# First feed-forward in pieces of 384 tokens across pairs of batches, weight products in rows of 16 array tiles, and new plan times

## The chip, the cores and the metric

The kernel runs on one core of one Trainium2 chip. The metric is the device time of one execution in microseconds (us). The engines of the core are TensorE (PE in the rows; PEld is its weight load), VectorE (DVE), ScalarE (ACT), GpSimd (POOL) and SyncE (SP); the last two also issue transfers.

## The reference

Three stages follow each other. Packed attention: 32 learned queries `p` attend to 576 keys of each head, and the 576 queries attend to the 32 results. Then two feed-forwards run over 8 x 576 = 4608 tokens of width 512.

```python
# B, H, S, D = 8, 8, 576, 64; 32 packed queries
p_packed = softmax(p @ k.T / 8) @ v
out = softmax(q @ p_packed.T / 8) @ p_packed
x = out.transpose(0, 2, 1, 3).reshape(4608, 512)
h = x @ w_in                            # 512 x 2048
x = (h * sigmoid(1.702 * h)) @ w_out    # 2048 x 512
h = max(x @ w1, x @ w2, x @ w3)         # 512 x 768 each
out = h @ w_out2                        # 768 x 512
```

All data are fp32.

## The kernel before

**Precision.** A matmul in fp32r is done three times, on high and low parts of both operands: `mm3` (lines 111 to 115) issues low x high, high x low and high x high into one PSUM bank. Each of the three has its own weight load. Matmuls on plain fp32 data (scores, `pv`, `pw`) run as two passes on TensorE.

**Attention.** A `Group(b, g)` is four heads of a batch. Its small matmuls use a part of the array, 64 rows by 32 columns. Its result `at[b, g]` is not the attention's output but the second softmax (32 weights per head), transposed and split in high and low. The product with the packed values is moved into the weights: `pw_unit` (line 449) multiplies the packed values `sp[b, g]` of a batch with a quarter `n` of `w_in` (512 of 2048 hidden features) and so makes `pw[b, n]`, which the first feed-forward uses in place of `w_in`. A call makes this for both batches of a pair and one head group `g`: eight matmuls of 64x32 array tiles, one PSUM bank of 512 columns for each batch from the pool `ps_a` (two banks, tag `pa`). ScalarE copies a bank out as the high part, VectorE subtracts for the low part (`evac`, line 145). For pair 0, `wi` is the converted weight; for later pairs it is fetched again from DRAM by `load_wi` on GpSimd's queue into one of four `x` tiles.

**First feed-forward.** A unit `n` is a piece of tokens by 128 hidden features. `h_unit` (line 514) makes h for the piece with two `mm3`, one per head group, in one of two banks of `ps_h` (tag `ph`), and applies the GELU; `g_unit` splits it; `out_unit` (line 542) does four `mm3` into the four banks `c0` to `c3` of `ps_c`, which collect over the units of a run. A piece is half a batch, `HALF` = 288 tokens, so a batch has 32 units and the stage has 256. `PAT` and `PP` (lines 481 to 501) set the runs; batches 0, 1 and 7 are cut in runs of hidden features whose parts are added by VectorE (line 559). A finished run goes to DRAM (`x2d`) in one transfer.

**Order.** The order is a plan: `add(t, fn)` notes a step with a time in us that is only a key, and at the end all steps are sorted by it and issued (line 1022). The tables at the top (lines 33 to 48) set these times; `tn[n]` is the planned time of unit `n`. The output of unit `n-2` stands behind h of unit `n`. The weight products of a quarter are planned `Q_` or `R_` units ahead of their first use, the two head groups one or three units apart (lines 945 to 952). Engines run their instructions in the order issued.

**Second feed-forward.** It runs from about 749 us to the end, over blocks of 768 tokens, with weights that `Piece` (line 604) converts and combines during the late units of the first. Its matmuls have 384 columns (`p` in the rows) and 512 (`accb`).

Of the kernel before, what the change touches and what calls it, by code (L numbers as in the profile page):

```python
# [8 lines left out]
F32 = mybir.dt.float32  # L9
# [16 lines left out]
NFC = DFF // P  # L26
NF2 = DFF2 // P
# [17 lines left out]
B4_ = [20, 9.69, 1.29, 38.74]
PC_ = [-5.59, 5.97, 8.06, 6.97, 10.65, 15.48, 10.04, 11.93]
G_ = [15, 33, 97, 136, 183]
X_ = [252, 2.6]
PAIR0 = 1


@with_exitstack
def tile_packed_attention_moe(
# [395 lines left out]
    def pw_unit(bs, pr, g, n):  # L449
        w = wi[pr, g, n]  # L450
        os = {}
        for b in bs:
            if (b, n) not in pw:
                pw[b, n] = w_tile(f"pw_{b}_{n}")
            os[b] = pa_tile(f"pw_{b}_{g}_{n}")
# [8 lines left out]
        for b in bs:  # L464
            o = os[b]
# [7 lines left out]


# [17 lines left out]
    PP = []  # L492
    for b in range(2, B, 2):
        PP += {
            0: [(b, 0, 16), (b + 1, 0, 16)],
            1: [(x, y, y + 4) for x in (b, b + 1) for y in range(0, 16, 4)],
            2: [(x, y, y + 8) for x in (b, b + 1) for y in range(0, 16, 8)],
            3: [(x, y, y + 8) for y in range(0, 16, 8) for x in (b, b + 1)],
            4: [(x, y, y + 4) for y in range(0, 16, 4) for x in (b, b + 1)],
        }[0]  # L500
    PP[-1:] = [(B - 1, x, x + 4) for x in range(0, 16, 4)] if 4 == 4 else [(B - 1, x, x + 8) for x in range(0, 16, 8)] if 4 == 8 else PP[-1:]
    for b, f0, f1 in PAT + PP:
# [372 lines left out]
    def main():  # L875
# [204 lines left out]
```

## Time and profile before

| | before |
|---|---|
| median of 3 runs | 1297.01 us (1295.29 to 1297.29) |
| profiled execution, its own time | 1295.06 us |
| span from the first to the last instruction | 1293.3 us |
| granted TensorE clock, mean | 0.997 |
| TensorE matmuls | 1272.8 us busy (98%), 9990 |
| VectorE, ScalarE, GpSimd busy | 841.8, 522.7, 78.2 us |

The span is what one execution shows between its first and last instruction; the execution's own time is 1.8 us more. A busy share says that some instruction of the engine was under way. TensorE's rows overlap, since a matmul starts while the one before it still drains, so the distance between starts tells the pace. All rows are of the one profiled execution, with times in us from the span's start.

### The profile page before, as it was taken

What the parts mean: (1) busy time and instruction counts of PE and PEld (TensorE: products, weight loads), DVE (VectorE), ACT (ScalarE), POOL (GpSimd) and SP (SyncE); (2) the same over time, 40 slices, a digit from 0 to 9 for tenths busy, and PEclk for the clock granted to TensorE, in tenths of its full rate; (3) what the DMA queues carried; (4) which work ended last, traced back from release to release, by engine and by line L of the source; (5) the groups of instructions that cost most, each with busy time, mean ns of one, the idle gap of its engine ahead of it and who ended that gap; (6) DMA issues with size and microseconds to landing.
All of it is one profiled execution on the core that took longest, in us unless ns stands there. A gap on an engine that the chain in (4) does not pass through costs nothing.

```text
span 1293.3 us, 24741 instructions
## 1 busy us (share of the span) xinstructions
PE 1272.8 (98%) x9990; PEld 1179.7 (91%) x9990; DVE 841.8 (65%) x1734; ACT 522.7 (40%) x1133; POOL 78.2 (6%) x153
## 2 busy tenths in 40 slices
PE   6999999999999999999999999999999999999998
PEld 5688888899989899999999999899899999998997
DVE  7998788565543466588789887557467366366561
ACT  3676654454654454455556532312213123113111
POOL 1000000000000000000000011011011011010100
PEclk8999999999999999999999999999999999999999
DMA  8898254323220231045557399567477477474541
GB/s 311 315 406 314 74 157 145 103 88 99 91 87 18 90 109 48 24 145 182 170 180 240 129 347 342 202 218 245 157 260 250 156 260 247 160 254 177 187 172 49
DMA packets 84402, 233.07 MB, mean 180 GB/s; under 512 B 9792, under 2 KB 38976, under 8 KB 77376
## 3 DMA queue, kind: packets, MB, share of 16 engines
q1 hardware_dynamic: 64128, 115.62, 26.0%
q0 software_dynamic: 20160, 115.88, 25.8%
q8 instruction: 78, 1.28, 0.4%
q14 instruction: 36, 0.29, 0.1%
HBM read 191.88 MB, written 39.58 MB: 179 GB/s over the span
## 4 chain that ended last, share of the span: by engine, by line
PE 88%; DVE 5%; DMA 3%; ACT 2%; issue 1%; SPq 0%; DVEq 0%; ACTq 0%
PE p L115 10%; PE p L114 10%; PE p L113 10%; PE acc L113 10%; PE acc L115 9%; PE acc L114 9%; PE h L113 5%; PE h L115 4%; PE h L114 4%; PE accb L115 4%; PE accb L114 4%; PE accb L113 4%; PE pw L460 2%; PE s L311 1%; DMA wraw_o<-in_w_out 1%; PE pv L366 1%
## 5 line engine op out<-in xcount | busy, mean ns | idle before, releaser
L113 PE MATMUL acc<-g,wo 128*128 128x288 f32 x1024 | 309.0, 302 | 1.9 <-DVE x L559 1.4
L115 PE MATMUL acc<-g,wo 128*128 128x288 f32 x1024 | 301.1, 294 | 0.0
L114 PE MATMUL acc<-g,wo 128*128 128x288 f32 x1024 | 299.4, 292 | 0.0
L113 PEld LDWEIGHTS acc<-g,wo 128*128 128x128 f32 x1024 | 192.2, 188 | 32.3 <-ACT t L526 11.9
L115 PEld LDWEIGHTS acc<-g,wo 128*128 128x128 f32 x1024 | 192.0, 188 | 1.4 <-issue 1.3
L114 PEld LDWEIGHTS acc<-g,wo 128*128 128x128 f32 x1024 | 192.3, 188 | 0.6 <-issue 0.5
L113 PE MATMUL h<-at,pw 128*128 128x288 f32 x512 | 154.0, 301 | 1.2 <-ACT at L142 0.6
L114 PE MATMUL h<-at,pw 128*128 128x288 f32 x512 | 151.5, 296 | 0.4 <-DVE at L143 0.4
L115 PE MATMUL h<-at,pw 128*128 128x288 f32 x512 | 151.3, 296 | 0.0
L113 PE MATMUL p<-x_T,ws 128*128 128x384 f32 x324 | 108.2, 334 | 0.0
L114 PE MATMUL p<-x_T,ws 128*128 128x384 f32 x324 | 108.2, 334 | 0.0
L115 PE MATMUL p<-x_T,ws 128*128 128x384 f32 x324 | 108.1, 334 | 0.0
L750 DVE TENSOR_TENSOR u<-s,p 128x384 f32<-128x384 f32 x54 | 29.9, 554 | 118.3 <-PE p L115 118.3
L113 PEld LDWEIGHTS h<-at,pw 128*128 128x128 f32 x512 | 96.1, 188 | 9.7 <-issue 5.0
L534 DVE TENSOR_TENSOR g<-t,g 128x288 fp32r<-128x288 f32 x130 | 58.9, 454 | 67.9 <-ACT g L533 67.0
L524 ACT ACTIVATE t<-h 128x288 f32<-128x288 f32 x130 | 53.3, 410 | 112.5 <-PE h L115 112.1
L114 PEld LDWEIGHTS h<-at,pw 128*128 128x128 f32 x512 | 96.1, 188 | 1.6 <-DVE t L527 0.8
L115 PEld LDWEIGHTS h<-at,pw 128*128 128x128 f32 x512 | 96.1, 188 | 0.5 <-issue 0.5
L780 ACT COPY s<-p 128x384 f32<-128x384 f32 x54 | 25.9, 480 | 164.5 <-PE p L115 164.5
L527 DVE SCALAR_TENSOR_TENSOR t<-t,h 128x288 f32<-128x288 f32 x126 | 56.8, 451 | 54.1 <-ACT t L526 53.4
L526 ACT ACTIVATE t<-h 128x288 f32<-128x288 f32 x126 | 51.8, 411 | 93.2 <-PE h L115 92.7
L115 PE MATMUL accb<-wo,g 128*128 128x512 f32 x216 | 84.1, 390 | 0.0
(166 smaller groups left out, 2587.7 us busy)
## 6 DMA issues: line engine op xcount, KB each, us to landing
ws<-wss POOLq DMA_DIRECT2D x54, 1024.0 KB, 7.5
wa<-wsa POOLq DMA_DIRECT2D x54, 768.0 KB, 4.6
wi<-wsc POOLq DMA_DIRECT2D x24, 512.0 KB, 3.7
k<-in_k SPq DMA_DIRECT2D x16, 576.0 KB, 4.0
q<-in_q SPq DMA_DIRECT2D x16, 576.0 KB, 4.1
x2d<-x SPq DMA_DIRECT2D x16, 576.0 KB, 3.6
wss<-ws SPq DMA_DIRECT2D x36, 256.0 KB, 2.9
xr<-x2d SPq DMA_DIRECT2D x24, 384.0 KB, 4.3
```

The source lines that it names most:

```text
L113: nc.tensor.matmul(o, al, bh, start=start, stop=False, skip_group_check=more)
L114: nc.tensor.matmul(o, ah, bl, start=False, stop=False, skip_group_check=more)
L115: nc.tensor.matmul(o, ah, bh, start=False, stop=stop, skip_group_check=more)
L311: self.mm = nc.tensor.matmul(o[hf][rows(c, r, hf ^ self.swap), :HALF], w(c, rows_in(r)), x[rows_in(r), c, hf * HALF:hf * HALF + HALF], sta ...
L366: self.mm = nc.tensor.matmul(o[h][m, :D], self.et[rows_in(h), c * P + NP * j:c * P + NP * j + NP], self.v[rows_in(h), c, d:d + D], start=c ...
L460: nc.tensor.matmul(os[b][rows(x, r, b & 1)], sp[b, g][rows_in(r), NP * c:NP * c + NP], w[rows_in(r), c], start=True, stop=True,)
L524: latest["act"] = nc.scalar.activation(t, o, AF.Gelu_apprx_sigmoid)
L526: nc.scalar.activation(t, o, AF.Tanh, scale=0.5 * 1.702)
L527: nc.vector.scalar_tensor_tensor(out=t, in0=t, scalar=1.0, in1=o, op0=ALU.add, op1=ALU.mult)
L534: latest["dve"] = nc.vector.tensor_tensor(out=g[:, 1], in0=gt[n], in1=f(g[:, 0]), op=ALU.subtract)
L750: latest["dve"] = nc.vector.tensor_tensor(out=o, in0=a, in1=b, op=op)
L780: latest["act"] = nc.scalar.copy(self.s1, self.b1)
```

## The change

- From batch 2 on the pieces of the first feed-forward are windows of `WIDE` = 384 tokens over a pair of batches: two batches of 576 tokens are three pieces. The middle piece holds the last 192 tokens of one batch and the first 192 of the other. As the two batches have different `pw`, its h is made in two parts of 192 columns in one bank; its output matmuls have 384. The units become 64 of 288 (batches 0 and 1, as before) and 144 of 384, 48 of these with h in two parts: 208 instead of 256. Per pair and chunk of 128 hidden features that is 60 matmuls instead of 72.
- The last two pieces are done in turns of four chunks each, with parts added by VectorE. A finished piece fills two `x` tiles and goes out in two transfers.
- `pw_both` issues the matmuls of both head groups behind each other, the first into the banks of `ps_a`, the second into those of `ps_h`, and copies all four banks out after that. It stands behind h of a unit and the output of the unit two before; the output of the unit just before is drawn ahead and stands directly behind it (`early`), and two h units follow each other later.
- `load_wi` is planned 10 and 8 units ahead of the product instead of 7.
- All plan times are new: conversions (`K_`, `L_`), attention of batch 0 (`D_`), the start of the units (`T_`), the weights of the second feed-forward (`TP_`, `PC_`), the units whose GELU is one ScalarE instruction (`G_`), and places that were unit numbers (`X_`, `U_`).

```diff
+WIDE = 384
-Q_ = [9, 8, 9, 8]
-R_ = [18, 26, 14, 8]
+Q_ = [6, 8, 7, 7]
+R_ = [14, 24, 12, 8]
-T_ = [41.76, 1.21, 1.17, 7]
+T_ = [40.26, 1.21, 1.17, 10]
...
+    def h_tile(name):
+        return ps_h.tile([P, TB], F32, tag="ph", name=name)
...
-    def pw_unit(bs, pr, g, n):
+    def pw_unit(bs, pr, g, n, tile_=pa_tile):
...
-            os[b] = pa_tile(f"pw_{b}_{g}_{n}")
+            os[b] = tile_(f"pw_{b}_{g}_{n}")
...
+        return lambda: pw_out(os, g, n)
+
+    def pw_out(os, g, n):
+        for b, o in os.items():
...
+    def pw_one(*a):
+        pw_unit(*a)()
+
+    def pw_both(bs, pr, n):
+        for done in [pw_unit(bs, pr, g, n, (pa_tile, h_tile)[g]) for g in range(2)]:
+            done()
...
+    def window(c0, width):
+        parts = []
+        for b in range(c0 // S, (c0 + width - 1) // S + 1):
+            t0, t1 = max(0, c0 - b * S), min(S, c0 + width - b * S)
+            parts.append((b, t0, t1 - t0, b * S + t0 - c0))
+        return c0, width, tuple(parts)
+
+    for b, f0, f1 in PAT:
         for hf in range(2):
...
+    runs = [(x, 0, NFC) for x in range(2 * S, NT, WIDE)]
+    runs[-2:] = [(x, y, y + 4) for y in range(0, NFC, 4) for x in range(NT - 2 * WIDE, NT, WIDE)]
...
     def h_unit(n):
-        b, hf, fc = units[n]
-        o = ps_h.tile([P, TB], F32, tag="ph", name=f"h_{n}")[:, :HALF]
+        (_, width, parts), fc = units[n]
+        o = ps_h.tile([P, TB], F32, tag="ph", name=f"h_{n}")[:, :width]
...
-        for g in range(2):
-            w = pw[b, fc // 4][:, g]
-            mm3(o, (w[:, 0, fs], w[:, 1, fs]), [t[:, hs] for t in at[b, g]], g == 0, g == 1)
+        for b, t0, num, to in parts:
+            for g in range(2):
+                w = pw[b, fc // 4][:, g]
+                mm3(
+                    o[:, to:to + num], (w[:, 0, fs], w[:, 1, fs]), [t[:, t0:t0 + num] for t in at[b, g]],
+                    g == 0, g == 1, len(parts) > 1,
+                )
...
+            if fc == NFC - 1 and dc % num == num - 1:
+                nc.sync.dma_start(x2d[:, dc + 1 - num:dc + 1, c0:c0 + width], x2[dc // num])
...
                 for g in range(2):
...
-                    add(max(tn[nn - 7] + .3, tp - 8), load_wi, pr, g, n)
-                    add(max(tn[nn] + .3, tp), pw_unit, (2 * pr, 2 * pr + 1), pr, g, n)
+                    add(max(tn[nn - 10 + 2 * g] + .3, tp - 8, saved[g, n]), load_wi, pr, g, n)
+                add(tn[nn] + hu[nn] / 2 + .02, pw_both, (2 * pr, 2 * pr + 1), pr, n)
+                early.add(nn - 1)
+
+        for n in range(N1):
+            add(tn[n], h_unit, n)
+            add(tn[n + 1] + hu[n + 1] / 2 + .03 if n in early else tn[n + 2] + hu[n + 2] / 2, out_unit, n)
+            add(tn[n] + hu[n] / 2 + .01, g_unit, n)
```

The places in the order follow; numbers in the names are unit, batch, group or quarter, and a running number. On TensorE before, the h matmuls of the first unit of batch 2 (`h_64`; `at0` and `at1` are the high and low softmax):

```order
L113 MATMUL h_64_3290<-at0_2_0_2421,pw_2_0_2980 128x288
L114 MATMUL h_64_3290<-at1_2_0_2422,pw_2_0_2980 128x288
L115 MATMUL h_64_3290<-at0_2_0_2421,pw_2_0_2980 128x288
L113 MATMUL h_64_3290<-at0_2_1_2908,pw_2_0_2980 128x288
L114 MATMUL h_64_3290<-at1_2_1_2909,pw_2_0_2980 128x288
L115 MATMUL h_64_3290<-at0_2_1_2908,pw_2_0_2980 128x288
```

On TensorE after, the h matmuls of unit 80, the first of the middle piece of batches 2 and 3:

```order
L119 MATMUL h_80_3946<-at0_2_0_2387,pw_2_0_3106 128x192
L120 MATMUL h_80_3946<-at1_2_0_2388,pw_2_0_3106 128x192
L121 MATMUL h_80_3946<-at0_2_0_2387,pw_2_0_3106 128x192
L119 MATMUL h_80_3946<-at0_2_1_2906,pw_2_0_3106 128x192
L120 MATMUL h_80_3946<-at1_2_1_2907,pw_2_0_3106 128x192
L121 MATMUL h_80_3946<-at0_2_1_2906,pw_2_0_3106 128x192
L119 MATMUL h_80_3946<-at0_3_0_2445,pw_3_0_3108 128x192
L120 MATMUL h_80_3946<-at1_3_0_2446,pw_3_0_3108 128x192
L121 MATMUL h_80_3946<-at0_3_0_2445,pw_3_0_3108 128x192
L119 MATMUL h_80_3946<-at0_3_1_2949,pw_3_0_3108 128x192
L120 MATMUL h_80_3946<-at1_3_1_2950,pw_3_0_3108 128x192
L121 MATMUL h_80_3946<-at0_3_1_2949,pw_3_0_3108 128x192
```

One group of six at 288 columns is, in a middle piece, two groups of six at 192, the first with batch 2's weights and the second with batch 3's.

On TensorE before, at the weight product of batches 6 and 7, first head group, first quarter (a row with x2 stands for two matmuls):

```order
L114 MATMUL h_174_7179<-at1_5_1_5246,pw_5_3_5637 128x288
L115 MATMUL h_174_7179<-at0_5_1_5245,pw_5_3_5637 128x288
L460 MATMUL pw_6_0_0_7190<-wi_3_0_0_6992,sp_6_0_5919 32x512 x2
L460 MATMUL pw_7_0_0_7192<-wi_3_0_0_6992,sp_7_0_6244 32x512 x2
L460 MATMUL pw_6_0_0_7190<-wi_3_0_0_6992,sp_6_0_5919 32x512 x2
L460 MATMUL pw_7_0_0_7192<-wi_3_0_0_6992,sp_7_0_6244 32x512 x2
L113 MATMUL acc_160_0_6828<-g_172_7149,wo12_1932 128x288
L114 MATMUL acc_160_0_6828<-g_172_7149,wo12_1932 128x288
L115 MATMUL acc_160_0_6828<-g_172_7149,wo12_1932 128x288
```

On TensorE after, at the same product:

```order
L120 MATMUL acc_144_3_6709<-g_147_6738,wo2_825 128x384
L121 MATMUL acc_144_3_6709<-g_147_6738,wo2_825 128x384
L466 MATMUL pw_6_0_0_6796<-wi_3_0_0_6427,sp_6_0_5582 32x512 x2
L466 MATMUL pw_7_0_0_6798<-wi_3_0_0_6427,sp_7_0_5832 32x512 x2
L466 MATMUL pw_6_0_0_6796<-wi_3_0_0_6427,sp_6_0_5582 32x512 x2
L466 MATMUL pw_7_0_0_6798<-wi_3_0_0_6427,sp_7_0_5832 32x512 x2
L466 MATMUL pw_6_1_0_6807<-wi_3_1_0_6508,sp_6_1_6118 32x512 x2
L466 MATMUL pw_7_1_0_6808<-wi_3_1_0_6508,sp_7_1_6409 32x512 x2
L466 MATMUL pw_6_1_0_6807<-wi_3_1_0_6508,sp_6_1_6118 32x512 x2
L466 MATMUL pw_7_1_0_6808<-wi_3_1_0_6508,sp_7_1_6409 32x512 x2
L119 MATMUL acc_144_0_6697<-g_148_6763,wo4_1313 128x384
L120 MATMUL acc_144_0_6697<-g_148_6763,wo4_1313 128x384
```

Before, four rows stand between h of unit 174 and the output of unit 172, and the second head group follows six units later; now both groups' eight rows stand between the outputs of units 147 and 148.

On VectorE before, at the copies of that product (`t` and `g` are GELU and split of a unit):

```order
L527 SCALAR_TENSOR_TENSOR t_174_7186<-t_174_7186,h_174_7179 128x288
L537 SCALAR_TENSOR_TENSOR g_174_7217<-t_174_7186,g_174_7217 128x288
L147 TENSOR_TENSOR pw_6_0_7189<-pw_6_0_0_7190,pw_6_0_7189 128x512
L147 TENSOR_TENSOR pw_7_0_7191<-pw_7_0_0_7192,pw_7_0_7191 128x512
L527 SCALAR_TENSOR_TENSOR t_175_7227<-t_175_7227,h_175_7220 128x288
L537 SCALAR_TENSOR_TENSOR g_175_7242<-t_175_7227,g_175_7242 128x288
L527 SCALAR_TENSOR_TENSOR t_176_7254<-t_176_7254,h_176_7247 128x288
L537 SCALAR_TENSOR_TENSOR g_176_7283<-t_176_7254,g_176_7283 128x288
```

On VectorE after:

```order
L548 SCALAR_TENSOR_TENSOR t_149_6775<-t_149_6775,h_149_6768 128x384
L558 SCALAR_TENSOR_TENSOR g_149_6792<-t_149_6775,g_149_6792 128x384
L153 TENSOR_TENSOR pw_6_0_6795<-pw_6_0_0_6796,pw_6_0_6795 128x512
L153 TENSOR_TENSOR pw_7_0_6797<-pw_7_0_0_6798,pw_7_0_6797 128x512
L153 TENSOR_TENSOR pw_6_0_6795<-pw_6_1_0_6807,pw_6_0_6795 128x512
L153 TENSOR_TENSOR pw_7_0_6797<-pw_7_1_0_6808,pw_7_0_6797 128x512
L548 SCALAR_TENSOR_TENSOR t_150_6844<-t_150_6844,h_150_6837 128x384
L548 SCALAR_TENSOR_TENSOR t_151_6857<-t_151_6857,h_151_6850 128x384
L558 SCALAR_TENSOR_TENSOR g_150_6847<-t_150_6844,g_150_6847 128x384
```

Two copies stood between units 174 and 175; now four stand together, and the GELUs of the next two units, 150 and 151, follow each other behind them.

## Rows read from the trace of the kernel before

**Rows 1.** The page: busy time of the engines, and one transfer's time to landing.

```profile
PE 1272.8 (98%) x9990; PEld 1179.7 (91%) x9990; DVE 841.8 (65%) x1734; ACT 522.7 (40%) x1133; POOL 78.2 (6%) x153
...
wi<-wsc POOLq DMA_DIRECT2D x24, 512.0 KB, 3.7
```

**Rows 2.** Busy time by stretch: length, each engine's, PEclk, DMA share, GB/s.

```profile
0.00:49.00 49.00, 35.86 (x568) 24.66 (x569) 39.07 (x83) 25.01 (x58) 3.53 (x15) 0.93 0.89 324
49.00:136.00 87.00, 85.69 (x738) 75.92 (x736) 80.24 (x141) 56.42 (x113) 3.47 (x6) 1.00 0.85 323
136.00:560.00 424.00, 422.19 (x4323) 380.40 (x4321) 248.74 (x578) 206.51 (x502) 12.41 (x23) 1.00 0.28 89
560.00:728.00 168.00, 167.39 (x1298) 162.84 (x1291) 141.82 (x327) 98.74 (x217) 1.61 (x3) 1.00 0.57 191
```

**Rows 3.** Order in time (start, length, instruction), TensorE: first matmuls, five units apart.

```profile
640.28 0.29 PE L113 MATMUL h<-at,pw 128*128 128x288 f32 x1
...
652.15 0.29 PE L113 MATMUL h<-at,pw 128*128 128x288 f32 x1
```

**Rows 4.** Order in time, TensorE, second feed-forward: two matmuls, 18 apart.

```profile
849.78 0.33 PE L114 MATMUL p<-x_T,ws 128*128 128x384 f32 x1
...
852.90 0.33 PE L114 MATMUL p<-x_B,ws 128*128 128x384 f32 x1
```

**Rows 5.** Order in time, weight loads at two places behind short matmuls.

```profile
503.32 0.48 PEld L347 LDWEIGHTS t<-ident,e 128*128 128x128 f32 x4
503.77 0.19 PEld L113 LDWEIGHTS h<-at,pw 128*128 128x128 f32 x1
503.88 0.19 PEld L114 LDWEIGHTS h<-at,pw 128*128 128x128 f32 x1
...
512.34 0.19 PEld L113 LDWEIGHTS h<-at,pw 128*128 128x128 f32 x1
512.45 0.19 PEld L114 LDWEIGHTS h<-at,pw 128*128 128x128 f32 x1
```

**Rows 6.** Order in time, a unit with a weight product and its copies.

```profile
546.65 0.29 PE L113 MATMUL h<-at,pw 128*128 128x288 f32 x1
...
547.52 1.09 PE L460 MATMUL pw<-wi,sp 64*32 64x512 f32 x16
...
548.54 0.40 PE L113 MATMUL acc<-g,wo 128*128 128x288 f32 x1
...
549.57 1.29 DVE L147 TENSOR_TENSOR pw<-pw,pw 128x512 fp32r<-128x512 f32 x2
...
550.23 0.29 PE L113 MATMUL h<-at,pw 128*128 128x288 f32 x1
```

**Rows 7.** Order in time, TensorE, 548.2 to 548.7: the same product's second pass.

```profile
547.98 0.64 PE L460 MATMUL pw<-wi,sp 64*32 64x512 f32 x8
```

**Rows 8.** Order in time: two late copies, the first and the last.

```profile
208.15 0.40 PE L113 MATMUL acc<-g,wo 128*128 128x288 f32 x1
...
211.41 0.68 DVE L147 TENSOR_TENSOR pw<-pw,pw 128x512 fp32r<-128x512 f32 x1
...
617.22 0.41 PE L113 MATMUL acc<-g,wo 128*128 128x288 f32 x1
...
619.49 1.28 DVE L147 TENSOR_TENSOR pw<-pw,pw 128x512 fp32r<-128x512 f32 x2
```

**Rows 9.** TensorE's waits (total, times, longest): 48 to 135, 135 to 800, 0 to 48.

```profile
PE pw L460 <- DVE pw L147: 0.8, 1, 0.8
...
PE acc L113 <- DVE x L559: 1.4, 2, 0.8
...
PE t L347 <- ACT e L333: 3.4, 4, 1.4
```

**Rows 10.** Order in time, TensorE: the first output matmul of the first feed-forward.

```profile
48.86 0.29 PE L113 MATMUL acc<-g,wo 128*128 128x288 f32 x1
```

More of the change, by code (lines that the diff above doesn't have):

```diff
@@ L491, in tile_packed_attention_moe @@
     units, first, last = [], {}, {}
[L492 to L502, printed above, removed]
+    def window(c0, width):
[5 more added lines that the diff above has]
+    for b, f0, f1 in PAT:
         for hf in range(2):
             first[len(units)] = last[len(units) + f1 - f0 - 1] = 1
-            units += [(b, hf, fc) for fc in range(f0, f1)]
+            units += [(window(b * S + hf * HALF, HALF), fc) for fc in range(f0, f1)]
+    runs = [(x, 0, NFC) for x in range(2 * S, NT, WIDE)]
+    runs[-2:] = [(x, y, y + 4) for y in range(0, NFC, 4) for x in range(NT - 2 * WIDE, NT, WIDE)]
+    for c0, f0, f1 in runs:
+        first[len(units)] = last[len(units) + f1 - f0 - 1] = 1
+        units += [(window(c0, WIDE), fc) for fc in range(f0, f1)]
     start = {}
-    for n, (b, hf, fc) in enumerate(units):
-        start.setdefault((b, fc // 4), n)
+    for n, ((_, _, parts), fc) in enumerate(units):
+        for b, *_ in parts:
+            start.setdefault((b, fc // 4), n)
     part = {}
@@ L530, in g_unit @@
     def g_unit(n):
-        g = gp.tile([P, 2, HALF], F32R, tag="g", name=f"g_{n}")
+        g = gp.tile([P, 2, WIDE], F32R, tag="g", name=f"g_{n}")[:, :, :units[n][0][1]]
         if direct(n):
@@ L542, in out_unit @@
     def out_unit(n):
-        b, hf, fc = units[n]
+        (c0, width, _), fc = units[n]
         w = wo[fc]
@@ L549, in out_unit @@
             ds_ = slice(dc * P, dc * P + P)
-            o = acc[dc][:, :HALF]
+            o = acc[dc][:, :width]
             mm3(o, (w[:, 0, ds_], w[:, 1, ds_]), (g[:, 0], g[:, 1]), n in first, n in last)
@@ L883, in main @@
         attention(A_[3], 1, 1, AS_[3], 0)
-        N1 = 2 * B * NFC
+        N1 = len(units)
         tn = [0.0] * 300
+        early = set()
         t = T0
+        hu = [HU * (units[min(n, N1 - 1)][0][1] / HALF) for n in range(N1 + 2)]
         for n in range(N1 + 2):
             tn[n] = t
-            if n < N1:
-                add(t, h_unit, n)
-            if n >= 2:
-                add(t + HU / 2, out_unit, n - 2)
-            if n < N1:
-                add(t + HU / 2 + .01, g_unit, n)
-            t += (T_[1] * HU) if n < T_[3] else HU * T_[2]
+            t += hu[n] * (T_[1] if n < T_[3] else T_[2])
         TB0 = t
@@ L938, in main @@
         for pr in range(1, B // 2):
-            b0 = 64 * (pr - 1)
+            b0 = start[2 * pr - 2, 0]
             for idx, (b, g) in enumerate([(0, 0), (1, 0), (0, 1), (1, 1)]):
```

99 lines of the change are left out of this document (55 added, 44 removed).

## Prediction

> **What bounds the kernel now.** I read the page's busy shares first, then the busy time by stretch, the order in time of TensorE around single units, and last the list of waits. TensorE is busy for 98% of the span [rows 1], and in every stretch after the first 49 us it is busy almost without a hole, while VectorE has 59% and ScalarE 49% of the stretch from 136 to 560 us [rows 2]. Busy TensorE time is no measure of pace, since one row of 0.29 us covers the start of the next; the distance from start to start is. Five units of the first feed-forward (6 matmuls into h and 12 into acc, 288 columns each) take 652.15 - 640.28 = 11.87 us [rows 3], so a unit takes 2.374 us and a matmul of 288 columns 131.9 ns. In the second feed-forward 18 matmuls of 384 columns take 852.90 - 849.78 = 3.12 us [rows 4], 173.3 ns each. So the bound is TensorE's stream: 120 ns of 2.4 GHz columns plus 12, or 160 plus 13. The granted clock is 1.00 in every stretch after the first [rows 2]; it decides nothing here. A change pays by fewer or shorter TensorE intervals, or it doesn't pay.
>
> **Columns of the pieces, the largest term.** Take one pair of batches and one chunk of 128 hidden features. Before: four units, 72 matmuls of 288 columns, 4 x 2.374 = 9.496 us. After: three pieces, of which the middle one spans two batches, and its h is made of 12 matmuls of 192 columns; 48 matmuls have 384 columns. The columns are the same, 12 matmuls are gone. The 48 cost 48 x 173.3 = 8.318 us. No row shows a matmul of 192 columns with 128x128 weights. Its lower bound is the line through the two paces, 131.9 - 96 x (173.3 - 131.9) / 96 = 90.5 ns; its upper bound is the pace of 288 columns, 131.9. Between these lies the weight load, which every matmul has. Four loads for transposes of 128 columns start at 503.32, and the next ones at 503.77 and 503.88: 0.56 us for five, the first under a matmul of 288 columns (0.13), so 0.108 each; behind the short matmuls of another step one starts at 512.34 and the next at 512.45, 0.11 apart [rows 5]. Under a stream of 288 columns the load is hidden; under 80 ns of columns it is not. I take 109 ns, since these rows are of the same weights' shape and show loads with nothing else to wait for. Then a chunk costs 8.318 + 12 x 0.109 = 9.626 us, 0.130 more than before, and 16 chunks by 3 pairs give 48 x 0.130 = **+6.2 us**. The break-even is (9.496 - 8.318) / 12 = 98 ns. With 90.5 ns the term is 48 x (8.318 + 1.086 - 9.496) = -4.4; with 131.9 it is +19.5.
>
> **Two products in one row, the second term.** A weight product pw (64x32 array tiles, two passes) makes its unit 550.23 - 546.65 = 3.58 us long against 2.374, so it costs 1.21 us [rows 6]. Its second pass starts 547.98 - 547.52 = 0.46 us after the first [rows 6, 7], so two passes are 0.92 and 0.29 us is paid once per call: the array is emptied before and after, and the first full weight load stands open. The change puts both head groups' products into one row of 16 tile matmuls; the second group goes to the two h banks. The 0.29 is then paid once instead of twice. In the new order 14 of the 15 pairs of calls stand directly behind each other (batches 0 and 1 with the second quarter of the hidden features do not): 14 x 0.29 = **-4.1 us**. The ends are 0, if the second group starts only when the array is empty, and -4.1 less a tenth for rounding.
>
> **What the second group's banks cost.** This is an added wait. The two units behind a call need the h banks back, and they get them when ScalarE and VectorE have copied the second group out. Queued behind the waiting h matmul on TensorE is everything else. At 547 us the call ends at 548.54 and VectorE has copied both banks by 549.57 + 1.29 = 550.86, 2.32 us later [rows 6]. In a row of 16 the first group is done 0.92 earlier, and its third copy comes 0.645 after the second: 2.32 - 0.92 + 0.645 = 2.05 us after the end. The cover is the output unit that the plan now puts directly behind the row: 0.11 + 12 x 0.1733 = 2.19 us, or 0.11 + 12 x 0.1319 = 1.69 in the four merged calls among units of 288. So 0.14 us are to spare in ten calls, and 0.36 are short in four, of which two have a second output unit or a score step as cover. But in seven of the 24 calls of the later pairs the copies came late, over 3 us behind the call: at the first of the seven the call ends at 208.15 and the copy at 211.41 + 0.68 = 212.09 (3.94 us), at the last at 617.22 and 619.49 + 1.28 = 620.77 (3.55 us) [rows 8]. A call as late as the last would wait 3.55 - 0.92 + 0.645 - 2.19 = 1.1 us. In the new order only two calls have weight conversions of the second feed-forward in front of their copies. I take 2 x 0.36 + 1.1 = **+2**; the ends are 0 and 14 x 1.1 = +15. In exchange the one wait of a second group for the banks of the first, 0.8 us between 48 and 135 us [rows 9], goes: **-0.8**.
>
> **The start and the rest of the plan.** The new times move the keys of batch 0's second group ahead of its first group's values (576 KB) and a load of 1024 KB of output weights ahead of batch 1. At 324 GB/s [rows 2] these are 1.8 us earlier on the chain that starts the first feed-forward and 3.2 us later for batch 1, whose scores stand on TensorE ahead of the first h now. The first output matmul starts at 48.86 [rows 10]; I take **-1** for it, with ends of -1.8 and +3.2. Work that costs nothing: 48 fewer copies, GELUs and subtractions on ScalarE and VectorE (cover: their idle share, 41% and more to 560 us); if it were gone they would set the pace, as VectorE with 142 of 168 us nearly does from 560 to 728 us [rows 2]. Each piece now stores two tiles instead of one by SP; the weights that pw reads are fetched 10 and 8 units ahead on GpSimd's queue instead of 7, some 30 us, against a landing of 3.7 us [rows 1]. Both use the four x tiles; a late one would cost one call's start. The two waits of output matmuls for VectorE's additions, 1.4 us together [rows 9], stay: the same additions stand there. The second feed-forward has the same instructions at the same pace.
>
> **Sum.** The profiled execution took 1295.06 us (span 1293.3 and 1.8 around it); the median of the runs is 1297.01, 1.95 more. 1295.06 + 6.2 - 4.1 + 2 - 0.8 - 1 = 1297.4, and on the median's side 1299.3. I say **1299.2 us**. A measurement of this kernel tells 0.2%, 2.6 us, from no change, so this is just inside "the same" (1294.4 to 1299.6).
>
> **Rivals.**
> (a) Matmuls of 192 columns keep the pace of their columns, 90.5 ns: the weight loads overlap. The term is -4.4 instead of +6.2, so 1288.6. Against it stands that loads next to each other never start closer than 0.108 in [rows 5]. Chance 0.08. The Trainium skill (TensorE: Matmul & The Clock Gate, Back-to-back issue gap) gives N/2.4 + 2.5 ns for an isolated gap, 82.5 ns for 192, and by it the term would be -9.0 and the time 1284; the trace does not bear the formula out here, since it gives 122.5 for 288 columns where the rows have 131.9.
> (b) The new plan is better than I can read from an order: the start gains its 1.8 us, no h bank is waited for, and the waits of 1.4 us for VectorE's additions go. Then 1299.2 - 0.8 - 2 - 1.4 - 1 for smaller holes = 1294.0. For it: in the first 48 us TensorE waits 3.4 us for exponentials alone [rows 9], and an order can reach that. Against it: after 49 us [rows 9] leave little to win. Chance 0.20.
> (c) Slower: the h matmul behind each row of 16 waits for its bank. It decides from the point where VectorE's third copy ends later than 2.19 us after the row; at half of a late call's wait, 14 x 0.55 = 7.7 instead of 2, it is 1304.9. For it: a margin of 0.14 us only. Against it: in the new order the four copies stand together directly behind the GELU's work. Chance 0.16. The Trainium skill (TensorEngine Tiling (Array Packing), Performance Considerations, PSUM Bottleneck) warns of just this, that tiling speeds up TensorE but not the emptying of PSUM.
> (d) The change doesn't do what it says: the row of 16 is run as two rows of 8 with the array emptied between. The gain of 4.1 is gone: 1303.3. Chance 0.08.
>
> **How the numbers follow.** My forecast has 0.48, with a range of its own from 1295.5 to 1302.5; 0.27 of it lies within 0.2% and 0.19 above, 0.02 below. (a) and 0.14 of (b) are faster, 0.06 of (b) the same; (c) and (d) are slower, save 0.01. Faster by over 0.2%: 0.24; within: 0.34; slower: 0.42. The range for 8 in 10 is 1291 to 1305: it leaves out (a), the far part of (c), and little at either end of (b).
>
> **What would show it.** In the profile of the changed kernel: matmuls of 192 columns that start 0.108 to 0.112 apart, with their weight loads as far apart (90 would be (a)); units of 384 of 18 x 0.1733 = 3.12 us, and of 3.39 us in the middle pieces; a row of 32 tile passes some 1.9 us long, and a unit with one longer by 2.1 us (2.4 would be (d)); no wait of h for pw's copies over 0.4 us (over 1 us in most rows would be (c)); the first output matmul about 1 us before 48.86. I am wrong if 192 columns cost less than 98 ns or more than 120, or if the part up to 136 us moves by more than 3 us.

## The result

The changed kernel takes **1309.51 us** (median of 4 runs, 1308.76 to 1310.19), the kernel before 1296.37 (median of 4): ratio **1.0102, 95% interval 1.0084 to 1.0119**. It is 13 us slower. The prediction was 1299.2 with a range of 1291 to 1305, so the time lies outside it.

The page and the busy time by stretch of the changed kernel answer to [rows 1, 2]: length, then busy time of PE, PEld, DVE, ACT and POOL, PEclk, DMA share, GB/s. The last two lines are short stretches inside the fourth.

```profile
PE 1281.0 (98%) x9414; PEld 1191.7 (91%) x9414; DVE 839.4 (64%) x1666; ACT 511.2 (39%) x1035; POOL 78.3 (6%) x153
...
0.00:49.00 49.00, 34.67 (x561) 25.36 (x562) 39.79 (x83) 25.32 (x58) 3.57 (x15) 0.90 0.95 345
49.00:136.00 87.00, 86.66 (x727) 77.00 (x727) 77.15 (x133) 55.59 (x110) 3.52 (x6) 1.00 0.81 299
136.00:560.00 424.00, 421.21 (x3972) 381.26 (x3972) 239.28 (x523) 200.84 (x443) 12.46 (x24) 1.00 0.28 90
560.00:728.00 168.00, 161.76 (x1017) 157.29 (x1017) 142.93 (x311) 87.75 (x171) 0.50 (x1) 0.98 0.52 174
...
707.00:713.20 6.20, 0.93 (x9) 0.75 (x7) 4.66 (x13) 3.25 (x6) 0.00 (x0) 0.88 0.94 327
713.20:718.40 5.20, 5.15 (x18) 5.18 (x19) 5.17 (x11) 1.35 (x4) 0.00 (x0) 0.50 0.65 208
```

The page's share for TensorE is 98% again and says nothing. The stretches do: from 560 to 728 us TensorE was busy 167.39 us before [rows 2] and is busy 161.76 now, and the hole is in one place. The order in time of TensorE there (start, length, instruction, and in brackets the idle time ahead and what ended it):

```profile
706.53 0.28 PE L120 MATMUL h<-at,pw 128*128 128x192 f32 x1
...
707.54 0.27 PE L120 MATMUL h<-at,pw 128*128 128x192 f32 x1
707.65 0.27 PE L121 MATMUL h<-at,pw 128*128 128x192 f32 x1
713.25 0.66 PE L119 MATMUL acc<-g,wo 128*128 128x384 f32 x1 [5.33 <-DVE x L584]
713.71 0.52 PE L120 MATMUL acc<-g,wo 128*128 128x384 f32 x1
714.03 0.52 PE L121 MATMUL acc<-g,wo 128*128 128x384 f32 x1
714.35 0.52 PE L119 MATMUL acc<-g,wo 128*128 128x384 f32 x1
```

TensorE waits 5.33 us for additions on VectorE (L584: they add an accumulation of four chunks to the part that stands in x2, and give back its bank). Behind the wait the matmuls of 384 columns start 0.32 us apart, where they are 0.173 otherwise, and the stretch shows a granted clock of 0.50, the lower level of 1.2 GHz. What VectorE did meanwhile:

```profile
707.24 0.41 DVE L611 TENSOR_SCALAR c_o<-wraw_o 128x512 int32<-128x512 int32 x1
...
709.73 0.43 DVE L611 TENSOR_SCALAR c_o<-wraw_o 128x512 int32<-128x512 int32 x1 [1.54 <-DMA wraw_o<-in_w_out]
...
711.95 0.68 DVE L614 SCALAR_TENSOR_TENSOR c_o<-wraw_o,c_o 128x512 f32<-128x512 uint16 x1
712.55 1.94 DVE L584 TENSOR_TENSOR x<-acc,x 128x384 f32<-128x384 f32 x4
```

It converts w_out2 (L611 to L620, six instructions, some 3 us, for each of six parts, 0 to 5). The order on each engine is fixed when the program is built; in it most of part 3 and the first three instructions of part 4 stand ahead of the four additions, and part 4 was still on its way from memory (1.54 us of the wait). The set of four additions before this one stands at 691.98; between the two sets VectorE ran 23 instructions of these conversions. In the kernel before, 12 stand between the sets at the same place, and TensorE isn't held there. The sets before the stall, first after and then before:

```profile
691.98 2.12 DVE L584 TENSOR_TENSOR x<-acc,x 128x384 f32<-128x384 f32 x4
...
702.48 1.54 DVE L559 TENSOR_TENSOR x<-acc,x 128x288 f32<-128x288 f32 x4
...
711.94 1.55 DVE L559 TENSOR_TENSOR x<-acc,x 128x288 f32<-128x288 f32 x4
```

**Where the 15 us are.** The profiled executions took 1310.19 and 1295.06 us, 15.1 apart, where the medians are 13.1 apart. From the first matmul of the second feed-forward on, the two traces are equally long; it starts 15.0 us later (764.15 against 749.12). Each interval from one matmul's start to the next can be given to the kind of the first, with idle time of over 0.08 us apart. The sums up to that point, as differences to the kernel before, in us (e16, e8 and e12 are experiments below):

```
                                   after   e16_spread  e8_nocross  e12_r10one
h and acc (columns and clock)       +8.3      +5.8        -8.6        -0.6
pw (weight products)                -3.2      -3.2        -3.5        -1.9
idle                                +7.0      +2.3        +1.2        +0.1
attention, transposes and filler    +2.9      +1.5        +3.1        -0.7
together                           +15.0      +6.4        -7.8        -3.1
```

### The profile page after: what moved, and what is told of

Same layout as the page of the kernel before. It is cut to its first block, busy times and chain, and to the rows that moved or that the text cites. A ratio compares the mean times of both kernels' runs of the same rounds, so it can differ in the third digit from the quotient of the medians.

```text
span 1308.4 us, 23350 instructions
## 1 busy us (share of the span) xinstructions
PE 1281.0 (98%) x9414; PEld 1191.7 (91%) x9414; DVE 839.4 (64%) x1666; ACT 511.2 (39%) x1035; POOL 78.3 (6%) x153
## 3 DMA queue, kind: packets, MB, share of 16 engines
q8 instruction: 74, 1.21, 0.4%
## 4 chain that ended last, share of the span: by engine, by line
PE 89%; DVE 5%; DMA 3%; ACT 2%; issue 1%; SPq 0%; POOL 0%; ACTq 0%; DVEq 0%; POOLq 0%
PE p L121 10%; PE p L120 10%; PE p L119 10%; PE acc L119 9%; PE acc L121 9%; PE acc L120 9%; PE h L119 5%; PE h L120 5%; PE h L121 5%; PE accb L121 4%; PE accb L120 4%; PE accb L119 4%; PE pw L466 2%; PE s L317 1%; PE pv L372 1%
## 5 line engine op out<-in xcount | busy, mean ns | idle before, releaser
L119 PE MATMUL acc<-g,wo 128*128 128x384 f32 (+1 forms) x832 | 272.9, 330 | 6.6 <-DVE x L584 5.6
L121 PE MATMUL acc<-g,wo 128*128 128x384 f32 (+1 forms) x832 | 269.0, 324 | 0.0
L120 PE MATMUL acc<-g,wo 128*128 128x384 f32 (+1 forms) x832 | 268.7, 323 | 0.0
L119 PEld LDWEIGHTS acc<-g,wo 128*128 128x128 f32 x832 | 156.1, 188 | 25.0 <-issue 9.9
L119 PE MATMUL h<-at,pw 128*128 128x384 f32 (+2 forms) x512 | 157.6, 308 | 3.5 <-ACT at L148 2.5
L120 PEld LDWEIGHTS acc<-g,wo 128*128 128x128 f32 x832 | 156.9, 189 | 1.4 <-DVE g L555 0.8
L121 PEld LDWEIGHTS acc<-g,wo 128*128 128x128 f32 x832 | 156.7, 188 | 0.1
L120 PE MATMUL h<-at,pw 128*128 128x384 f32 (+2 forms) x512 | 155.7, 304 | 0.0
L121 PE MATMUL h<-at,pw 128*128 128x384 f32 (+2 forms) x512 | 155.3, 303 | 0.0
L119 PEld LDWEIGHTS h<-at,pw 128*128 128x128 f32 x512 | 97.1, 190 | 14.2 <-issue 6.2
L548 DVE SCALAR_TENSOR_TENSOR t<-t,h 128x384 f32<-128x384 f32 (+1 forms) x112 | 57.2, 512 | 66.9 <-ACT t L547 66.5
L120 PEld LDWEIGHTS h<-at,pw 128*128 128x128 f32 x512 | 97.4, 190 | 1.3 <-DVE at L149 0.8
L121 PEld LDWEIGHTS h<-at,pw 128*128 128x128 f32 x512 | 97.5, 190 | 0.0
L547 ACT ACTIVATE t<-h 128x384 f32<-128x384 f32 (+1 forms) x112 | 51.5, 461 | 106.6 <-PE h L121 106.1
L555 DVE TENSOR_TENSOR g<-t,g 128x384 fp32r<-128x384 f32 (+1 forms) x96 | 50.8, 531 | 61.7 <-ACT g L554 61.4
L121 PE MATMUL accb<-wo,g 128*128 128x512 f32 x216 | 84.1, 390 | 0.0
L120 PE MATMUL accb<-wo,g 128*128 128x512 f32 x216 | 84.1, 390 | 0.0
```

The source lines that it names most:

```text
L119: nc.tensor.matmul(o, al, bh, start=start, stop=False, skip_group_check=more)
L120: nc.tensor.matmul(o, ah, bl, start=False, stop=False, skip_group_check=more)
L121: nc.tensor.matmul(o, ah, bh, start=False, stop=stop, skip_group_check=more)
L547: nc.scalar.activation(t, o, AF.Tanh, scale=0.5 * 1.702)
L548: nc.vector.scalar_tensor_tensor(out=t, in0=t, scalar=1.0, in1=o, op0=ALU.add, op1=ALU.mult)
L555: latest["dve"] = nc.vector.tensor_tensor(out=g[:, 1], in0=gt[n], in1=f(g[:, 0]), op=ALU.subtract)
```

## The experiments

Theory S at first: 8.5 us of columns, -4 for rows of 16, 7 for the stall and its clock, 2 for small waits. The other letters in the expectations are O (the order of VectorE's work makes the stall) and the rivals F (VectorE has too much work there), Q (the late load makes it), P (the early numbers matter), M (rows of 16 bring nothing net) and C (192 columns go by their columns). All ratios are to the kernel before, with 95% intervals. The edits are cut to the lines that matter.

**e8_nocross: a middle piece takes all its 384 tokens from the first of its two batches.** It leaves out the h of the second batch's tokens in these pieces.

```diff
+        if len(parts) > 1:
+            parts = [(parts[0][0], S - width, width, 0)]
```

> The changed kernel, in which a piece that crosses two batches takes all its 384 tokens from the first of the two: 6 matmuls of 384 columns into h in place of 12 of 192, everything else as it was. It computes other values for these tokens. Theory S (192 columns run at the pace of the weights, 112.8 ns apart in the changed kernel where 384 are 173.3): each of the 48 middle units is shorter by 12 x 0.1128 - 6 x 0.1733 = 0.314 us, 15 us in all, and the time falls to 1294 to 1297 us, with the stall near 707 us still there (some 15 us earlier). Rival F (VectorE and the plan hold the middle of the kernel, columns are only a part): less than 9 us.

1287.09 us, 0.9927 (0.9912 to 0.9942): 22.4 us less than the changed kernel. h and acc give 14.4 of it against the run with no stall (+5.8 to -8.6), as expected (15). The other 8 are the stall and its clock, which are gone, and that was not expected: the time is 7 us under the expected range. Busy time by stretch and TensorE's wait for the additions (total, times, longest):

```profile
540.00:708.00 168.00, 168.00 (x1041) 162.31 (x1041) 142.61 (x312) 91.21 (x178) 2.09 (x4) 1.00 0.52 174
...
PE acc L119 <- DVE x L586: 0.3, 1, 0.3
```

VectorE does the same work, 142.61 of 168 us, and TensorE is never held. In this program's order the additions stand ahead of parts 3 and 4: matmuls that are shorter changed the order that was worked out. So VectorE being full is not enough for the stall.

**e5_400: a pair cut into 400, 400 and 352**, the middle piece of 176 and 224 columns.

```diff
-    runs = [(x, 0, NFC) for x in range(2 * S, NT, WIDE)]
+    cuts = [(x + y, z) for x in range(2 * S, NT, 2 * S) for y, z in ((0, 400), (400, 400), (800, 352))]
+    runs = [(x, 0, NFC) for x in cuts]
...
```

> The changed kernel with a pair of batches cut into 400, 400 and 352 tokens, so that the middle piece takes 176 columns from one batch and 224 from the other. Theory S (narrow matmuls go at the pace of their weights, 0.109 to 0.113 us, whatever their columns): 176 and 224 columns both 0.108 to 0.116 us apart. Rival C (they go by their columns and a fixed part): 176 columns 0.10 us or less, 224 columns 0.125 us or more, in proportion to 112.8 ns for 192.

One run, 1311.07 us. Order in time, TensorE, one middle unit:

```profile
298.44 0.27 PE L120 MATMUL h<-at,pw 128*128 128x176 f32 x1
...
298.89 0.27 PE L121 MATMUL h<-at,pw 128*128 128x176 f32 x1
...
299.14 0.27 PE L120 MATMUL h<-at,pw 128*128 128x224 f32 x1
...
299.58 0.28 PE L121 MATMUL h<-at,pw 128*128 128x224 f32 x1
```

Four steps of 176 columns take 0.45 us, four of 224 take 0.44: 0.11 each whatever the columns, as S expects; C falls. In the changed kernel 9 steps of 192 take 1.01 us (706.53 to 707.54 above), 0.112 each.

**e4_apart: rows of 16 taken apart into two rows of 8.**

```diff
-                add(tn[nn] + hu[nn] / 2 + .02, pw_both, (2 * pr, 2 * pr + 1), pr, n)
+                for g in range(2):
+                    add(tn[max(nn - 2 * (1 - g), start[2 * pr, 0] - 8)] + .3, pw_one, (2 * pr, 2 * pr + 1), pr, g, n)
...
```

> The changed kernel with the rows of 16 taken apart again: two rows of 8 for each quarter of the weights, on two banks each, from batch 0 on where the first group's row is drawn 2 units ahead; pieces of 384 and all numbers of the plan stay. Theory S (a row of 16 saves 0.4 us as measured in quiet stretches: of the run with rows of 16 alone and pieces of 288, between units 63 and 160, 2.1 us for 5 rows without the one that waited): 5 us more than the changed kernel, 1313 to 1316 us. Rival M (what a row saves is lost again where its banks and copies come late): within 2 us of the changed kernel.

1325.02 us, 1.0221 (1.0206 to 1.0236), 15.5 us above the changed kernel. The direction is right and the size isn't: of the 24 rows of the later three pairs 9 took 0.2 to 2.1 us longer than the others (1.29 us from the matmul ahead to the one behind), some of them with a wait for the copies of an accumulation or for an attention step. It shows that a row's place matters as much as its length, and gives no clean price.

**e2_merge and e3_288: pieces of 288 with rows of 16**; e2 with the early numbers of before, e3 with the new ones.

```diff
-WIDE = 384
+WIDE = 288
...
-U_ = [180, 200, 201, 202, 1.46]
+U_ = [225, 240, 248, 249, 2]
```

> The kernel before with rows of 16 alone: pieces of 288 tokens, and every number of the plan as before, the early ones too. Theory S (early plan worth nothing): the same as the run with the early plan set anew, 1291.5 to 1293.5 us. Rival P (the new early plan gives or takes something, which the second group's later weights hide): more than 2 us apart from that run, in either direction.

> The changed kernel with the pieces of 384 tokens taken back to 288 (no piece then crosses two batches), and with the plan's numbers that count units of the first feed-forward, and those of the late stretch, as before; rows of 16 and the early plan stay. Theory S: the rows of 16 give back 0.3 us at each of 14 places and the early plan is worth nothing, so 1291.5 to 1293.5 us where the kernel before gives 1296.4, and 16 to 17 us less than the changed kernel (8.5 for columns, 7 for the stall and its clock, 2 for smaller waits). Rival M (rows of 16 bring nothing net, since their copies and banks cost what they give): 1296 to 1297.5 us.

e2: 1298.01 us, 1.0015 (1.0005 to 1.0025). e3: 1301.83 us, 1.0038 (1.0024 to 1.0051). Both miss S; e3 against the changed kernel gives 7.7 us and not 16 to 17. The early plan set anew costs 3.8 us in a kernel of 288 (P's side). For the rest e2's trace shows rows of 16 in the way of others, in order of time on TensorE:

```profile
433.62 1.06 PE L466 MATMUL pw<-wi,sp 64*32 64x512 f32 x8
434.98 1.05 PE L466 MATMUL pw<-wi,sp 64*32 64x512 f32 x4 [0.30 <-ACT e L339]
436.20 1.94 PE L466 MATMUL pw<-wi,sp 64*32 64x512 f32 x20 [0.17 <-ACT e L339]
438.06 0.40 PE L119 MATMUL acc<-g,wo 128*128 128x288 f32 x1
...
615.75 0.40 PE L119 MATMUL h<-at,pw 128*128 128x288 f32 x1 [1.36 <-DVE pw L153]
```

One row, 1.95 us elsewhere, is held by a softmax and takes 4.4; behind another the next h waits 1.36 us for the copies that free its bank, which is rival (c) at one place.

**e9_r7, e9_r10, e9_r5: rows of 16 moved away from that, late conversions held back.** Base: pieces of 288, all numbers of before, rows of 16 in the later three pairs. The last number of R_ is 7, 10 and 5; the edit of R_ is shown against the kernel before.

```diff
-R_ = [18, 26, 14, 8]
+R_ = [18, 26, 14, 7]
...
+            with tc.issue_after(latest["add"].ins) if self.k > 6 else ExitStack():
                 self.v, self.s = conv_late(self.n, self.raw, *self.hl, TB)
```

> The kernel before (pieces of 288, all its numbers) with rows of 16 for the later three pairs alone, the last row of each pair one unit later than a straight carry-over, so that it misses the softmax that held it for 2.6 us at 434 us, and the last two pieces' conversions on VectorE queued behind the additions drawn ahead of them, where 2.6 us were lost at 727 us. Theory S (a row of 16 saves 0.38 us, 2.48 - 2.10, and loses only where banks or copies come late): 12 rows give 4.6 us, 1290 to 1293 us where before gives 1296.5. Rival M (each gain is lost again elsewhere): 1295.5 to 1298 us.

> As the run with the last row of each pair one unit later, but two units earlier than a straight carry-over. Theory S: 1290 to 1293 us if the row stands clear of the softmax and its copies; with a wait of 1 to 3 us at the row, 1292 to 1296 us.

> As the run with the last row of each pair one unit later, but three units later than a straight carry-over, 2 units of the first feed-forward (4.75 us) ahead of the first unit that needs its weights. Theory S: 1290 to 1293 us; if the second group's copies come too late for that unit (they ended 2.4 us behind a row), up to 2 us more at each of two places.

1297.93 (1.0020, 1.0006 to 1.0034), 1297.30 (1.0010, 1.0001 to 1.0018) and 1300.25 us (1.0036, 1.0025 to 1.0048): all three miss S. With R_ at 10 the first feed-forward ends 4.4 us earlier than before, and the second is 7.9 us longer. TensorE's waits of e9_r10:

```profile
PE p L119 <- DVE u L774: 2.4, 1, 2.4
PE p L119 <- ACT s L804: 2.1, 1, 2.1
```

The conversions held back now stand in front of the first set of the second feed-forward. It is the hold that costs this, not the rows: the next two runs are without it.

**e15_r10free and e12_r10one: no hold, and a hold of one place.**

```diff
+            with tc.issue_after(latest["add", 243].ins) if 2 * self.k + self.kc > 14 else ExitStack():
                 self.v, self.s = conv_late(self.n, self.raw, *self.hl, TB)
```

> The kernel before with rows of 16 for the later three pairs, the last row of each pair two units earlier than a straight carry-over, and nothing held back on VectorE. Up to unit 240 it should be as the run with the pieces held back (2.6 us ahead of the kernel before); then the additions behind a conversion that waits for its load cost up to 2 us at 727 us, and the second feed-forward starts without the 7.9 us that the pieces held back cost it. Theory S: 1293 to 1296 us. Rival M (what the rows give is lost at the change-over to the second feed-forward whatever stands there): 1296.5 us or more.

> As the run with nothing held back, but the conversion that waited for its load at 724 us queued behind the one set of additions that it held up (after units 240 to 243), so that it moves by some 2 us only. Theory S with O: the stall at 727 us gone, the second feed-forward as long as before, and the rows' 4.6 us show in the whole: 1290 to 1293 us. Rival M: 1295 us or more.

1293.52 us, **0.9978** (0.9968 to 0.9988), and 1292.04 us, **0.9967** (0.9957 to 0.9977), within S for both. e12 is the fastest here, 4.2 us under the kernel before. Its waits of TensorE from 136 to 765 us and its stretch from 560 to 728:

```profile
PE acc L119 <- DVE x L584: 1.2, 1, 1.2
PE h L119 <- DVE pw L153: 0.7, 3, 0.2
...
560.00:728.00 168.00, 167.79 (x1303) 164.25 (x1302) 142.65 (x328) 99.19 (x218) 1.08 (x2) 1.00 0.56 187
```

**e1_hold, e11_hold34, e6_queue, e10_light, e13_tp82, e14_tp11: the stall.** Hold all conversions of w_out2 behind the additions drawn ahead of them; hold parts 3 and 4 alone; load w_out2 from GpSimd's queue; leave its conversion out; draw the late work earlier; draw it farther apart. The six edits in this order:

```diff
+        with tc.issue_after(latest["add"].ins):
             conv_late(f"o{fc}", wo2[fc], w[:, 0], w[:, 1], TB)
...
+        with tc.issue_after(latest["add", 191].ins) if fc in (3, 4) else ExitStack():
             conv_late(f"o{fc}", wo2[fc], w[:, 0], w[:, 1], TB)
...
-        nc.sync.dma_start(raw, w_out2[fc])
+        nc.gpsimd.dma_start(raw, w_out2[fc])
...
-        conv_late(f"o{fc}", wo2[fc], w[:, 0], w[:, 1], TB)
+        h = f(wo2[fc]).rearrange("p (a w) -> p a w", w=2)[:, :, 1]
+        nc.scalar.copy(w[:, 0], h)
+        nc.vector.tensor_tensor(out=w[:, 1], in0=h, in1=f(w[:, 0]), op=ALU.subtract)
...
-TP_ = [8.85, 9.26, 9.39]
-U_ = [180, 200, 201, 202, 1.46]
+TP_ = [8.85, 8.2, 9.39]
+U_ = [170, 200, 201, 202, 1.46]
...
-TP_ = [8.85, 9.26, 9.39]
+TP_ = [8.85, 9.26, 11]
```

> The changed kernel, with one edge of order more: each conversion of a piece of w_out2 on VectorE is queued behind the last additions to x2 that the plan draws ahead of it. Nothing else is edited. Theory S (the changed kernel lost 5.3 us at 707.7 because the four additions stood behind two conversions in VectorE's queue, and some 2 us more because the granted clock was down after it): the wait of the output matmuls there falls to under 1 us, the clock stays up, and the time is 7 us less than the changed kernel's on the same chip, 1301 to 1304 us. Rival F (VectorE is too full in this stretch, 143 us of 168, so that the wait only moves to the next additions or to the start of the second feed-forward): a wait of 3 us or more elsewhere after 690 us, and 1306 to 1310 us.

> The changed kernel with two conversions alone held back: pieces 3 and 4 of w_out2 are queued on VectorE behind the additions of the accumulation that stalled (units 188 to 191), all others stay. The run without crossing pieces has put those additions two conversions earlier of itself and showed no wait there, with VectorE as full (142.6 us of 168). Theory O (order, not the amount of VectorE's work, makes the stall): the wait at 707 us falls under 1 us, at most 2 us of waits come later, and the time falls by 5 to 7.5 us to 1302 to 1305 us. Rival F (the pieces held back only make the next additions late, as when all were held): a wait of 3 us or more between 715 and 760 us, and within 3 us of the changed kernel.

> The changed kernel with the loads of w_out2 issued from GpSimd's queue in place of SyncE's, so that no load of them stands behind the stores and the loads of x. Theory S (the order on VectorE makes the stall; the load that came late is 1.5 us of it): the conversions still stand ahead of the additions, the wait shrinks from 5.3 us to 3 or 4, and the time falls by 1 to 2.5 us. Rival Q (the late load is the cause): the wait falls under 1.5 us and the time by 5 us or more.

> The changed kernel with the conversion of w_out2 left out but for one copy on ScalarE and one subtraction on VectorE (in place of 2 and 6): some 16 us of VectorE's work less in the last 60 us of the first feed-forward, and w_out2 isn't converted from its 64-bit form. Theory F (that stretch is bound by VectorE's work as such, so that the time lost at the stall can't be won back by another order): the wait for the additions falls under 1 us, no other wait of over 1 us takes its place, and the time falls by 7 to 9 us to 1301 to 1303 us. Theory O (the order is at fault: the additions stand behind whatever conversion is ahead of them): the wait only shrinks with the conversions' length, to 2 us or so, and the time falls by 3 to 5 us.

> The changed kernel with two numbers of the late plan alone: the conversions of the second feed-forward's weights are drawn 8.2 us apart in place of 9.26, and those of w_out2 from unit 170 in place of 180, so that the same work on VectorE stands some 15 us earlier and the conversions of w_out2 are shared out over more accumulations (in the program's order 4, 2, 0 begin ahead of the three additions that follow units 187, 191 and 195, where it was 2, 3 and 1). Theory O (order and place of VectorE's work make the stall): no wait of over 1.5 us between 690 and 765 us, and 1301 to 1304 us. Rival F (VectorE has no room for this work beside the first feed-forward, wherever it stands): waits of 4 us or more in all after 560 us, and 1307 us or more.

> The changed kernel with one number of the late plan: the conversions of w_out2 drawn 11 us apart in place of 9.39. In the program's order conversions 4 and 5 then begin behind the additions that stalled, with 3 whole ahead of them. Theory O: the wait at 707 us shrinks from 5.3 us to 2 or less, but with two conversions ahead of the next additions some of it comes back at 720 us: 1304 to 1307 us. Rival F: 1308 us or more.

```
            us        ratio (95%)                    first feed-forward ends, against after
e1_hold     1312.07   1.0119 (1.0104 to 1.0133)      -1.5
e11_hold34  1307.17   1.0079 (1.0065 to 1.0093)      -3.1
e6_queue    1311.45   1.0115 (1.0102 to 1.0128)      +0.6
e10_light   1316.52   1.0151 (1.0130 to 1.0171)      +6.1
e13_tp82    1315.95   1.0157 (1.0137 to 1.0177)      +5.4
e14_tp11    1309.76   1.0103 (1.0085 to 1.0121)      +0.9
```

None gives the time that S or O expects. In e1 the stall is gone and the units behind it are 7.3 us earlier, as S says; in the last five units of the stage 5.9 of it are lost again, with a wait of 2.7 us for additions, and the second feed-forward is 2.7 us longer. In e11 the wait for additions falls to 0.3 us, but a wait of 2.5 us for a GELU comes behind it. e6 does not test Q: its loads come later still, VectorE waits 3.13 us for one ahead of the additions, and TensorE's wait grows. Waits for additions of e1, then e6 with its load:

```profile
PE acc L119 <- DVE x L584: 2.9, 2, 2.7
...
707.70 0.43 DVE L611 TENSOR_SCALAR c_o<-wraw_o 128x512 int32<-128x512 int32 x1 [3.13 <-DMA wraw_o<-in_w_out]
...
PE acc L119 <- DVE x L584: 7.2, 2, 6.8
```

What speaks against Q is the changed kernel's own row: the load is 1.54 of the 5.33 us. e13 and e14 come out as F expects (waits of 7.4 us in all after 560 us, and one of 5.7 us that stays). e10 is the plainest: with five of six instructions of each conversion gone from VectorE, the time goes up, since another order is worked out that holds TensorE at two other places (its waits from 136 to 765 us):

```profile
PE acc L119 <- DVE x L584: 4.3, 2, 4.0
PE h L119 <- ACT t L545: 3.9, 1, 3.9
```

So the amount of work alone is not the cause: against F stand e8, e10 and the next run.

**e16_spread: two conversions between each pair of accumulations.**

```diff
+        with tc.issue_after(latest["add", 191 if fc < 4 else 195].ins) if fc > 1 else ExitStack():
             conv_late(f"o{fc}", wo2[fc], w[:, 0], w[:, 1], TB)
```

> The changed kernel with the conversions of w_out2 shared out by edges of order on VectorE: 0 and 1 ahead of the additions that stalled (after units 188 to 191), 2 and 3 behind them, 4 and 5 behind the next (after 192 to 195); nothing else is edited. Theory O (the order makes the stall): no wait of over 2 us between 690 and 765 us and 1301 to 1304 us. Rival F (with pieces that cross batches there is no room for this work ahead of the second feed-forward): waits of 4 us or more in all from 690 us to the second feed-forward's first set, and 1306 us or more.

1302.43 us, 1.0050 (1.0036 to 1.0063), 7.1 us less than the changed kernel, as O expects. TensorE's waits for VectorE's additions from 136 to 800 us, and the stretch of the stall:

```profile
PE acc L119 <- DVE x L584: 0.3, 1, 0.3
...
690.00:740.00 50.00, 50.00 (x324) 50.00 (x323) 44.65 (x90) 25.23 (x48) 1.08 (x2) 1.00 0.60 194
```

TensorE is never held in these 50 us while VectorE works 44.65 of them. Nine and twelve conversion instructions stand ahead of the two sets of additions there, where the changed kernel has 23 ahead of one. With the same instructions and four conversions held back by edges of order, the 7 us are gone (O); F, which expected 1306 us or more, falls.

## Why the prediction was wrong

- **The step that failed: "The two waits of output matmuls for VectorE's additions, 1.4 us together [rows 9], stay: the same additions stand there."** There are as many additions, 24 at the end of the stage, of 384 columns instead of 288; what stands in front of them is not the same. They cost 5.33 us of waiting, and some 2.5 us at the lower clock behind it (8.3 against 5.8 in the table), against 1.4 before [rows 9]. I had read that VectorE is at 142 of 168 us and had put the six conversions there, moved by the new plan, at nothing. e16 prices it at 7.1 us in the whole, or 6.4 when each kernel is set against the kernel before on its own chip. Without it the changed kernel stands at 1302.4, inside the range.
- **Columns, +6.2: right.** 192 columns are 0.112 apart (0.109 predicted) and not at the pace of their columns, so rival (a) falls. In e16, whose clock is undisturbed from 47 us on, h and acc are 5.8 us longer than before, with what they save behind fewer rows in it; e8 confirms the other side, 14.4 us for the crossing alone. The weight loads start as far apart as these matmuls, ten steps in 1.11 us:

```profile
706.45 0.19 PEld L120 LDWEIGHTS h<-at,pw 128*128 128x128 f32 x1
...
707.56 0.19 PEld L121 LDWEIGHTS h<-at,pw 128*128 128x128 f32 x1
```

  That the load sets this floor is argued from them and from e5; no run changes the load alone. The Trainium skill (TensorE: Matmul & The Clock Gate, LDWEIGHTS (loading the stationary operand)) states a load time of P / 1.2 ns for P columns, an estimate of 106.7 ns for 128, and the rows of 176, 192 and 224 columns with 110 to 112 ns agree.
- **Rows of 16, -4.1 +2 -0.8: right in the sum.** Order in time of one:

```profile
441.95 0.34 PE L121 MATMUL acc<-g,wo 128*128 128x384 f32 x1
442.22 1.95 PE L466 MATMUL pw<-wi,sp 64*32 64x512 f32 x32
444.10 0.44 PE L119 MATMUL acc<-g,wo 128*128 128x384 f32 x1
444.38 0.33 PE L120 MATMUL acc<-g,wo 128*128 128x384 f32 x1
```

  It makes the stream longer by 444.38 - 441.95 - 2 x 0.173 = 2.08 us, where two calls cost 2 x 1.21 [rows 6]: 0.34 saved, predicted 0.29. So (d) falls; (c) shows at single places only. pw's intervals are 3.2 us shorter in the changed kernel, and e12 and e15, which have rows of 16 and the old pieces, are 4.2 and 2.7 us faster than before.
- **The start, -1: wrong by some 2.** The first output matmul starts at 49.66 instead of 48.86 [rows 10], 0.8 later and not 1 earlier. The first h waits for the softmax and starts at 41.89 instead of 37.84, and the granted clock falls behind it. The first h and that stretch, the same part of the kernel before, and the first output matmul after:

```profile
41.89 0.53 PE L119 MATMUL h<-at,pw 128*128 128x288 f32 x2 [2.52 <-ACT at L148]
...
42.70:46.10 3.40, 3.40 (x24) 3.25 (x25) 3.23 (x6) 2.47 (x9) 0.00 (x0) 0.50 1.02 417
...
38.00:50.00 12.00, 10.12 (x203) 7.12 (x206) 11.50 (x27) 8.27 (x21) 0.00 (x0) 1.00 0.87 330
...
49.66 0.29 PE L119 MATMUL acc<-g,wo 128*128 128x288 f32 x1
```

  All twelve kernels with the new early numbers show such stretches at the lower clock, 3.4 to 10.2 us in all between 38 and 50 us, and none of the seven with the old ones does (before, e2, e9, e12, e15). That is part of what e3 loses against e2: its stretch is 10.2 us long, and its first output matmul stands at 51.90 against 49.27. With pieces of 384 the early numbers were not run by themselves.
- What is left between e16 and the kernel before on its own chip is 6.8 us; the table gives 5.8 - 3.2 + 2.3 + 1.5 = 6.4 for the profiled executions, 1.4 us of the idle time in the first 136 us. Which early number makes the holes there stays open.

## To carry to other kernels

A matmul whose columns take less time than the floor of its stream (here 0.11 us) pays the floor, so a wider piece that has to be cut in two at a border can cost more than it saves. When an edit changes the length of one engine's work, the order worked out for all engines changes with it: list what stands ahead of every instruction that frees a bank, at the fullest stretch of the helper engine, before calling it "the same". A gain that shows in a quiet stretch (here the rows of 16) is worth testing by itself: e12 keeps it, without the pieces, and beats both kernels.

## What the runs showed of the hardware that was not expected

- 176, 192 and 224 columns run at one pace, 0.110 to 0.112 us, while 288 run at 0.132 and 384 at 0.173.
- A wait of some microseconds costs more than itself: behind 5.33 us of idle TensorE the granted clock is 0.50 from the first matmul (713.25) to 718.4. In e11 it falls behind a wait of 2.5 us as well, in the waits and the stretch behind it:

```profile
PE h L119 <- ACT t L545: 2.5, 1, 2.5
...
719.70:723.00 3.30, 3.22 (x10) 3.23 (x11) 2.73 (x6) 2.31 (x6) 0.00 (x0) 0.51 0.59 196
```
